# 64 KB rows in three slots, one softmax per head: a decode attention kernel and its loads regrouped

## The chip, the cores and the metric

The kernel runs on one core of one Trainium2 chip. The metric is the device time of one execution in microseconds (us). The kernel before takes 709.22 us, the median of three runs (712.56, 709.22 and 707.17).

## What is computed

One decode step of grouped-query attention with a cache, gated by a small MLP. There are 8 batches of one token each, 32 query heads and 8 key/value heads of width 128, and 4096 cached positions. All data are float32.

```
xn = layernorm(x)                                  # x: (8, 1, 512)
q  = (xn @ wq) as (batch, 32 heads, 1, 128)        # wq: (512, 4096)
s  = q . k_cache * 128**-0.5                       # k_cache: (8, 8, 4096, 128), one kv head per 4 q heads
o  = softmax(s) . v_cache                          # v_cache: (8, 8, 4096, 128)
a  = o as (batch, 1, 4096) @ wo                    # wo: (4096, 512)
z  = gelu(xn @ w_in)                               # w_in: (512, 1792), z1 and z2 are its halves
y  = (z1 * (w_sp * layernorm(z2) + b_sp)) @ w_out  # w_out: (896, 512)
out = x + a * silu(y)
```

The two caches are 268.4 MB (2 x 8 x 8 x 4096 x 128 x 4 bytes); wq, wo, w_in and w_out are 8.39, 8.39, 3.67 and 1.84 MB. Each byte is read once.

## The kernel before

The work goes through 64 pairs of a kv head `h` and a batch `b`, heads outermost. A pair needs one K tile and one V tile of 2 MB: 128 partitions with a row of 16 KB each. Both come from the pool `kv` with six buffers. K lies in memory with the head dimension on the partitions (its layout is made on the host); V lies with positions on the partitions.

For a pair, `scores` (L203) multiplies the 4 query vectors of the pair (a 128x4 stationary operand) with K, in four column groups g of 32 output partitions each, of which 4 are used, and two chunks c of 512 positions. The result is one PSUM tile of 128x1024, whose 16 used rows hold 4 query heads x 4 groups. VectorE takes the negated maximum of each row (L205), ScalarE the exponential with the sum of each row (L207). `transposed` turns the result with eight 128x128 transposes on TensorE (L216) and copies the 16 used columns out (L217). `values` (L225) multiplies it with V, 32 times for a pair, and L227 copies the 128x128 result out. Since every row has its own maximum, `factors` rescales the four groups once a head (L232 to L249), `combine` sums them with a matmul for each batch (L254), and `project_o` adds the head's share of the output projection into `acc` (L261).

What TensorE executes is written in a loop with one pair of delay: the scores of pair i come ahead of the transposes and values of pair i-1 in program order. TensorE runs its matmuls in that order. The last three pairs (`TAIL`) are handled apart in `finish_last`: their scores come first, and the last V tile comes in eight pieces.

All large loads are issued from one queue (SP) in program order: K and V of a pair, `wo` of the head at b = 2 and `wq` of the next head at b = 4 (1 MB each, in rows of 2 KB), `w_in` at pair 9 and `w_out` at pair 12. A load into a `kv` buffer waits on SP until TensorE has read the tile that was there, and each load waits for one of eight completion semaphores (named DMAHW0 to DMAHW7 below), which are used in turn. Whatever follows on SP waits behind. The query projection of head h+1 stands after pair b = 6 (L119), the MLP after pairs 11 and 14 (L144, L184).

In the profile a float32 matmul counts as two instructions, so the 8 matmuls of a pair's scores are x16 and the 32 of its values x64.

## Time and profile before

| what | value |
|---|---|
| median of three runs | 709.22 us (707.17 to 712.56) |
| span of the profiled execution | 707.2 us |
| TensorE busy (matmul) | 497.6 us, 70% |
| VectorE, ScalarE busy | 149.0 us, 80.6 us |
| packets of the SP queue, as a share of 16 DMA engines | 98.4% |
| bytes read | 290.80 MB |
| mean TensorE clock granted | 0.81 |

The profile shows one execution by its span, from the first to the last instruction. No other time of that execution is shown, so the span is its own time here; it is the same as the fastest of the three runs (707.17 us) and 2.0 us under their median. Busy time is the union of an engine's instructions, so four matmuls that run beside each other in four column groups count once. A packet is one contiguous row that one of the 16 DMA engines moves, or the few bytes that count up a semaphore; the share of a queue is the sum of its packets' durations over 16 times the time looked at. Since the groups of a stage overlap with loads for others, the busy shares alone don't say which engine sets the time.

### The profile page before, as it was taken

To read this page: it belongs to the slowest core of one execution; us is meant where nothing else is said; L and a number is where in the kernel's file an instruction comes from. 1 tells how busy PE (TensorE), PEld (TensorE's weight loads), DVE (VectorE), ACT (ScalarE), POOL (GpSimd) and SP (SyncE) were. 2 spreads that over 40 slices of the span, in tenths; PEclk is the share of its full clock that TensorE was granted. 3 is DMA by queue.
4 is the path that set the end of the run, shared out by engine and by line. 5 is a ranking of instruction groups with operands and counts; after the bars stand their busy time and mean duration, and the time that the engine had idled before them with its cause. 6 is when DMAs were issued, how large, how long until landed. Compare 5 with 4: busy or idle time off the path is not lost.

```text
span 707.2 us, 14005 instructions
## 1 busy us (share of the span) xinstructions
PE 497.6 (70%) x6480; PEld 305.9 (43%) x6480; DVE 149.0 (21%) x364; ACT 80.6 (11%) x139; POOL 3.1 (0%) x10
## 2 busy tenths in 40 slices
PE   6656777787868668776867668686477764878666
PEld 4323454573534345344534334444144432545334
DVE  2211122112222221222122211222112221122231
ACT  0110101001010110011011100111010111001120
POOL 0000000000000000000000000000000000000000
PEclk9967788856777996789778977978877897677999
DMA  8999999999999999999999999999999999999994
GB/s 336 429 419 422 426 428 422 423 406 427 425 394 376 416 428 428 426 421 420 427 428 425 423 419 426 429 418 425 423 427 426 419 422 426 426 426 423 427 395 170
DMA packets 31178, 291.77 MB, mean 413 GB/s; under 512 B 2952, under 2 KB 3208, under 8 KB 14864
## 3 DMA queue, kind: packets, MB, share of 16 engines
q1 hardware_dynamic: 30672, 290.79, 98.4%
q8 instruction: 51, 0.84, 0.5%
q10 hardware_dynamic: 448, 0.08, 0.1%
q14 instruction: 7, 0.06, 0.0%
HBM read 290.80 MB, written 0.07 MB: 411 GB/s over the span
## 4 chain that ended last, share of the span: by engine, by line
PE 49%; DMA 33%; DVE 9%; ACT 7%; issue 1%; ACTq 0%; DVEq 0%; SPq 0%
DMA kv<-in_kT 30%; PE sc L203 16%; PE o_ps L225 14%; PE scr L216 8%; DVE nm L205 7%; ACT p L207 6%; PE scr L119 4%; PE scr L144 3%; DMA kv<-in_v 2%; PE scr L254 2%; DMA xg_sb<-in_xg 1%; PE acc L261 1%; PE scr L184 0%; PE scr L245 0%; DVE o_sb L227 0%
## 5 line engine op out<-in xcount | busy, mean ns | idle before, releaser
L216 PE MATMUL scr<-ident,p 128*128 128x128 f32 x512 | 85.3, 320 | 145.2 <-ACT p L207 144.6
L203 PE MATMUL sc<-kv,qT 128*4 128x512 f32 x1024 | 154.9, 732 | 27.5 <-DMA kv<-in_kT 27.2
L225 PE MATMUL o_ps<-kv,pT 128*4 128x128 f32 x4096 | 169.0, 332 | 1.7 <-DMA kv<-in_v 1.6
L216 PEld LDWEIGHTS scr<-ident,p 128*128 128x128 f32 x512 | 66.6, 162 | 210.4 <-ACT p L207 208.3
L225 PEld LDWEIGHTS o_ps<-kv,pT 128*4 128x4 f32 x4096 | 120.6, 103 | 42.4 <-DVE pT L217 8.0
L207 ACT ACTIVATE p<-sc,nm 128x1024 f32<-128x1024 f32 x64 | 71.2, 1113 | 535.3 <-DVE nm L205 476.3
L205 DVE TENSOR_REDUCE nm<-sc 128x1 f32<-128x1024 f32 x64 | 78.4, 1225 | 172.0 <-PE sc L203 172.0
L203 PEld LDWEIGHTS sc<-kv,qT 128*4 128x4 f32 x1024 | 26.3, 95 | 90.8 <-issue 56.2
L217 DVE COPY pT<-scr 128x64 f32<-128x64 f32 x128 | 28.6, 224 | 155.9 <-PE scr L216 155.9
L227 DVE COPY o_sb<-o_ps 128x128 f32<-128x128 f32 x64 | 18.7, 292 | 152.7 <-PE o_ps L225 152.7
L119 PEld LDWEIGHTS scr<-xnT,wq_sb 128*128 128x128 f32 x256 | 35.9, 227 | 2.3 <-issue 2.0
L119 PE MATMUL scr<-xnT,wq_sb 128*128 128x8 f32 x256 | 36.7, 284 | 0.3 <-DVE xnT L113 0.3
L254 PEld LDWEIGHTS scr<-f,o_sb 128*128 128x128 f32 x128 | 22.8, 267 | 19.1 <-issue 11.5
L254 PE MATMUL scr<-f,o_sb 128*128 128x4 f32 x128 | 24.3, 312 | 6.1 <-DVE f L249 5.3
L144 PEld LDWEIGHTS scr<-xnT,w_in_sb 128*128 128x128 f32 x112 | 19.0, 271 | 0.2 <-issue 0.2
L144 PE MATMUL scr<-xnT,w_in_sb 128*128 128x8 f32 x112 | 19.1, 315 | 0.0
L261 PE MATMUL acc<-wo_sb,oT 128*8 128x128 f32 x256 | 11.0, 327 | 4.8 <-DVE oT L258 4.8
L207 ACT ACTIVATION_READ_ACCUMULATOR p<-sc,nm 128x1 f32 x64 | 12.3, 193 | 0.0
L261 PEld LDWEIGHTS acc<-wo_sb,oT 128*8 128x8 f32 x256 | 7.0, 103 | 6.5 <-DVE oT L258 5.5
L122 DVE TENSOR_SCALAR qT<-scr 128x32 f32<-128x32 f32 x8 | 1.5, 192 | 34.0 <-PE scr L119 34.0
L245 PE MATMUL scr<-wl,same 128*128 128x8 f32 x16 | 2.9, 252 | 6.3 <-DVE wl L243 6.3
L241 ACT ACTIVATE w<-w 128x8 f32<-128x8 f32 x8 | 1.7, 208 | 37.5 <-DVE w L240 37.5
(67 smaller groups left out, 45.2 us busy)
## 6 DMA issues: line engine op xcount, KB each, us to landing
kv<-in_kT SPq DMA_DIRECT2D x62, 2048.0 KB, 23.8
kv<-in_v SPq DMA_DIRECT2D x61, 2048.0 KB, 21.3
wq_sb<-in_wq SPq DMA_DIRECT2D x8, 1024.0 KB, 23.1
wo_sb<-in_wo SPq DMA_DIRECT2D x8, 1024.0 KB, 22.7
kv<-in_kT SPq DMA_DIRECT2D x4, 1024.0 KB, 15.5
kv<-in_v SPq DMA_DIRECT2D x8, 512.0 KB, 16.6
w_in_sb<-in_w_in SPq DMA_DIRECT2D x4, 896.0 KB, 23.6
kv<-in_v SPq DMA_DIRECT2D x8, 256.0 KB, 7.0
```

Of the source, the lines that this page charges most:

```text
L119: nc.tensor.matmul(pq[:, r * B:(r + 1) * B], wq_sb[:, k, r * DH:(r + 1) * DH], xnT[:, k, :], start=(k == 0), stop=(k == NK - 1))
L144: nc.tensor.matmul(pz[:, f * B:(f + 1) * B], w_in_sb[:, k, f * P:(f + 1) * P], xnT[:, k, :], start=(k == 0), stop=(k == NK - 1))
L203: nc.tensor.matmul(s[32 * g:32 * g + REP, c, :], qT[:, b, :], k_sb[:, c, g, :], start=True, stop=True)
L205: nc.vector.tensor_reduce(nm[:, b:b + 1], s, op=ALU.max, axis=AX.XY, negate=True)
L207: nc.scalar.activation(p.rearrange("p j s -> p (j s)"), s.rearrange("p c s -> p (c s)"), AF.Exp, bias=nm[:, b:b + 1], accum_out=l[:, b:b + 1])
L216: nc.tensor.transpose(t[:, j * P:(j + 1) * P], p[:, 4 * c + j, :], ident)
L217: nc.vector.tensor_copy(pT[:, 4 * c:4 * c + 4], t.rearrange("p (j g r) -> p j g r", j=4, g=G)[:, :, :, :REP])
L225: nc.tensor.matmul(o_ps[32 * g:32 * g + REP, :], pT[:, j, g, :], v_sb[:, j, g, :], start=(j == 0), stop=(j == J - 1))
L227: nc.vector.tensor_copy(o_sb[:, b, :], o_ps)
L245: nc.tensor.matmul(tot, same.rearrange("p g r -> p (g r)"), wl, start=True, stop=True)
L254: nc.tensor.matmul(po[:, b * REP:(b + 1) * REP], stats[h][2][:, b, :], f[:, b, :], start=True, stop=True)
L261: nc.tensor.matmul(acc[32 * g:32 * g + B, :], oT[:, r, :], wo_sb[:, r, g * P:(g + 1) * P], start=(h == 0 and r == 0), stop=(h == HKV - 1 a ...
```

## The change

The caches are laid out anew on the host, so that one load brings four batches of K, or of V, of a head: 8.4 MB, 128 rows of 64 KB. The tile pool becomes a ring of three slots of 64 KB a partition, and everything large goes through it. `w_in` and `w_out` share the first slot, whose unused part also holds the MLP's intermediate tiles; all of `wq` is the second; then follow, for each head, K in two halves and V in two halves; all of `wo` is the last, in six pieces of 16, 8, 4, 2, 1 and 1 of its 32 rows of 2 KB a partition. The last V half comes in four pieces.

The MLP and the query projection of all heads are computed first. They now use the small operand `xnT`, padded to 32 columns, as the stationary one, and the weights as the moving one. The queries are written into `qz`, where the four queries of batch b stand in columns 4b to 4b+3 of a 32-column block that is zero elsewhere. So the scores of all eight batches add up into one PSUM tile `sc` whose 32 rows of a column group hold 8 batches x 4 heads, and one softmax a head serves all of them: one maximum, one exponential, eight transposes. The rescaling is applied to `p` ahead of its transposes. `combine` runs once a V half, and the output projection runs once at the end.

On SP, the start of the program, with the semaphores that each load waits for. Before (a `kv` tile is a K or V tile of a pair):

```order
L44 DMA wq_sb_122<-in_wq 128x4x512
L56 DMA kv_143<-in_kT 128x2048 x2
L64 DMA kv_146<-in_v 128x4096
L56 DMA kv_162<-in_kT 128x4096 [waits DMAHW0_49]
L64 DMA kv_164<-in_v 128x4096 [waits DMAHW1_49]
L56 DMA kv_223<-in_kT 128x4096 [waits DMAHW2_49]
L64 DMA kv_225<-in_v 128x4096 [waits DMAHW3_49]
L49 DMA wo_sb_227<-in_wo 128x4x512 [waits DMAHW4_49]
L56 DMA kv_286<-in_kT 128x4096 [waits DMAHW6_49,DMAHW5_49,PE_49]
```

And now (slot_77, slot_80 and slot_340 are the first use of the three slots):

```order
L56 DMA slot_77<-in_w_in 128x7168
L57 DMA slot_77<-in_w_out 112x4096
L67 DMA slot_80<-in_wq 128x16384
L257 DMA slot_340<-in_kT 128x16384
L257 DMA slot_374<-in_kT 128x16384 [waits DMAHW1_49,DMAHW3_49,DVE_49,PE_49]
L264 DMA slot_442<-in_v 128x16384 [waits DMAHW4_49,PE_49]
L264 DMA slot_580<-in_v 128x16384 [waits DMAHW5_49,DMAHW0_49,PE_49]
L257 DMA slot_718<-in_kT 128x16384 [waits DMAHW6_49,PE_49]
```

Four loads (22.3 MB) are now issued without a wait; the fifth waits for the MLP, which reads and writes the first slot, the sixth for the query projection, the seventh for the scores of the first K half.

On SP, the end of the program. Before, the last V tile in eight pieces of 2 KB rows:

```order
L64 DMA kv_4526<-in_v 128x1024 [waits DMAHW7_49]
L64 DMA kv_4542<-in_v 128x512 [waits DMAHW0_49,PE_49]
L64 DMA kv_4542<-in_v 128x512 [waits DMAHW1_49]
L64 DMA kv_4542<-in_v 128x512 [waits DMAHW2_49]
L64 DMA kv_4542<-in_v 128x512 [waits DMAHW3_49]
```

And now, from the last V half on:

```order
L264 DMA slot_3226<-in_v 128x4096 [waits DMAHW1_49,PE_49]
L264 DMA slot_3226<-in_v 128x4096 x3
L280 DMA slot_3231<-in_wo 128x8192 [waits DMAHW2_49,PE_49]
L280 DMA slot_3231<-in_wo 128x4096
L280 DMA slot_3231<-in_wo 128x2048
L280 DMA slot_3231<-in_wo 128x1024 [waits DMAHW3_49]
L280 DMA slot_3231<-in_wo 128x512 [waits DMAHW4_49]
L280 DMA slot_3231<-in_wo 128x512 [waits DMAHW5_49]
L299 DMA out_0<-res_3514 128x128 [waits DMAHW6_49,DVE_49]
```

The pieces of wo wait for semaphores of loads that lie three and more loads back (DMAHW3 is that of the first V half of the last head, DMAHW4 and DMAHW5 those of the first two pieces of the second), where a piece of the last V tile before waited for the load eight places ahead of it.

On TensorE, the stretch from one pair to the next before, in the middle of the program:

```order
L203 MATMUL sc0_97<-kv_471,qT_141 4x512 x8
L216 MATMUL scr_567<-ident_83,p_484 128x128 x4
L216 MATMUL scr_573<-ident_83,p_484 128x128 x4
L225 MATMUL o_ps_99<-kv_473,pT_566 4x128 x32
L203 MATMUL sc1_98<-kv_551,qT_141 4x512 x8
```

And now all of one head:

```order
L203 MATMUL sc_98<-slot_340,qz_91 32x512 x32
L203 MATMUL sc_98<-slot_374,qz_91 32x512 x32
L213 MATMUL scr_411<-ident_82,nm_122 1x128
L219 MATMUL scr_417<-ident_82,full_415 128x1
L226 MATMUL scr_424<-wl_422,same_93 128x1
L234 MATMUL scr_430<-ident_82,p_409 128x128 x4
L234 MATMUL scr_436<-ident_82,p_409 128x128 x4
L242 MATMUL o_ps0_99<-slot_442,pT_429 4x128 x128
L251 MATMUL scr_574<-same_93,o_sb_572 128x4 x4
```

A head has as many matmuls for scores (64) and values (256) as before, but 8 transposes where there were 64, and no score of the next head stands ahead of this head's values.

The diff, cut:

```diff
-TAIL = 3
+R = 32
+HALF = B // 2
+UNIT = 2 * G * 512
+SLOT = HALF * UNIT
+WO_PIECES = [(0, 16), (16, 24), (24, 28), (28, 30), (30, 31), (31, 32)]
...
-    wpool = ctx.enter_context(tc.tile_pool(name="wpool", bufs=2))
-    kv = ctx.enter_context(tc.tile_pool(name="kv", bufs=6))
-    work = ctx.enter_context(tc.tile_pool(name="work", bufs=2))
+    ring = ctx.enter_context(tc.tile_pool(name="ring", bufs=3))
+    work = ctx.enter_context(tc.tile_pool(name="work", bufs=1))
...
+    def slot():
+        return ring.tile([P, SLOT], F32, name="slot")
...
+    nc.sync.dma_start(mlp_slot[:, :NK * 2 * FH], w_in)
+    nc.sync.dma_start(w_out_sb, w_out)
...
+    wq_sb = slot()
+    nc.sync.dma_start(wq_sb, wq)
...
+    qz = const.tile([P, HKV, B * R], F32, name="qz")
+    nc.gpsimd.memset(qz, 0.0)
...
+    def mlp():
+        z = from_slot(P, 2 * FQ).rearrange("p (a f) -> p a f", a=2)
+        pz = scratch([P, 2 * FQ], "pz")
+        for part in range(2):
             for k in range(NK):
+                for g in range(G):
+                    lo = part * FH + g * FQ
+                    nc.tensor.matmul(pz[R * g:R * (g + 1), part * FQ:(part + 1) * FQ], xnT[:, k, :],
+                                     w_in_sb[:, k, lo:lo + FQ], start=(k == 0), stop=(k == NK - 1))
...
+    def project_q(quad):
+        pq = scratch([P, REP * DH], "pq")
+        for k in range(NK):
             for g in range(G):
+                lo = (quad * G + g) * REP * DH
+                nc.tensor.matmul(pq[R * g:R * (g + 1), :], xnT[:, k, :], wq_sb[:, k, lo:lo + REP * DH],
+                                 start=(k == 0), stop=(k == NK - 1))
+        q_sb = work.tile([P, REP * DH], F32, name="q_sb", tag="p")
+        nc.vector.tensor_scalar(q_sb, pq, float(DH) ** -0.5, None, op0=ALU.mult)
+        tq = scratch([P, REP * P], "tq")
+        for r in range(REP):
+            nc.tensor.transpose(tq[:, r * P:(r + 1) * P], q_sb[:, r * DH:(r + 1) * DH], ident)
...
+                nc.vector.tensor_copy(qz[:, h, o:o + REP], tv[:, :, g, b])
...
+    def scores(h, half, k_sb):
+        for i in range(HALF):
+            b = half * HALF + i
+            for c in range(2):
+                for g in range(G):
+                    nc.tensor.matmul(sc[R * g:R * (g + 1), c, :], qz[:, h, b * R:(b + 1) * R],
+                                     k_sb[:, i, c, g, :], start=(b == 0), stop=(b == B - 1))
+
+    def softmax(h):
+        m = nm[:, h:h + 1]
+        nc.vector.tensor_reduce(m, sc, op=ALU.max, axis=AX.XY, negate=True)
+        p = work.tile([P, J, P], F32, name="p")
+        nc.scalar.activation(p.rearrange("p j s -> p (j s)"), sc.rearrange("p c s -> p (c s)"), AF.Exp,
+                             bias=m, accum_out=l[:, h:h + 1])
+        a = scratch([1, P], "a")
+        nc.tensor.transpose(a, m, ident)
...
+        nc.vector.tensor_scalar(p, p, w, None, op0=ALU.mult)
+        pT = work.tile([P, J, P], F32, name="pT")
         for c in range(2):
             t = scratch([P, 512], "t")
             for j in range(4):
                 nc.tensor.transpose(t[:, j * P:(j + 1) * P], p[:, 4 * c + j, :], ident)
+            nc.vector.tensor_copy(pT[:, 4 * c:4 * c + 4, :].rearrange("p j s -> p (j s)"), t)
...
+    def load_k(h, half):
+        t = slot()
+        nc.sync.dma_start(t, kT[h, half])
...
+    mlp()
+    project_q(0)
+    project_q(1)
+    for h in range(HKV):
+        for half in range(2):
+            scores(h, half, load_k(h, half))
+        pT = softmax(h)
+        for half in range(2):
+            last = h == HKV - 1 and half == 1
+            v_sb = load_v(h, half, HALF if last else 1)
+            if last:
+                wo_slot = slot()
+                for lo, hi in WO_PIECES:
+                    nc.sync.dma_start(wo_slot[:, lo * D:hi * D], wo[:, lo * D:hi * D])
+            o = o_ps[half]
+            for i in range(HALF):
+                values(half * HALF + i, pT, v_sb[:, i], o)
+                if last:
+                    combine(h, half * HALF + i, 1, o)
+            if not last:
+                combine(h, half * HALF, HALF, o)
...
+    for m in range(HKV * REP):
+        h, r = divmod(m, REP)
+        for g in range(G):
+            nc.tensor.matmul(acc[R * g:R * g + B, :], oT[:, h, r, :], wo_sb[:, m, g * P:(g + 1) * P],
+                             start=(m == 0), stop=(m == HKV * REP - 1))
...
+        "kT": c(k.transpose(2, 0, 7, 1, 4, 6, 5, 3)).reshape(HKV, 2, P, SLOT),
+        "v": c(vv.transpose(2, 0, 3, 1, 4, 5, 6)).reshape(HKV, 2, P, SLOT),
+        "wq": c(c(A_wq).reshape(NK, P, HKV * REP * DH).transpose(1, 0, 2)).reshape(P, SLOT),
+        "wo": c(c(A_wo).reshape(HKV * REP, P, D).transpose(1, 0, 2)).reshape(P, SLOT),
```

More of the change, by code (lines that the diff above doesn't have):

```diff
@@ L85, in tile_gqa_gmlp_decode @@
         nc.vector.tensor_copy(same[:, g, :], same[:, 0, :])
-    sc = [ps_fix.tile([P, 2, 512], F32, name=f"sc{i}") for i in range(2)]
-    o_ps = ps_fix.tile([P, DH], F32, name="o_ps")
+    same_all = same.rearrange("p g r -> p (g r)")
+    sc = ps_fix.tile([P, 2, 512], F32, name="sc")
+    o_ps = [ps_fix.tile([P, HALF, DH], F32, name=f"o_ps{i}") for i in range(2)]
     acc = ps_fix.tile([P, P], F32, name="acc")
-    for t in (sc[0], sc[1], o_ps, acc):
+    for t in (o_ps[0], o_ps[1], acc):
         nc.vector.memset(t, 0.0)
@@ L126, in tile_gqa_gmlp_decode @@
[L126 to L148 removed]
+    nc.vector.tensor_copy(xnT[:, :, :B], pt.rearrange("p (k b) -> p k b", k=NK))
@@ L253, in combine @@
-    def combine(h, b, f, po):
-        nc.tensor.matmul(po[:, b * REP:(b + 1) * REP], stats[h][2][:, b, :], f[:, b, :], start=True, stop=True)
-    def project_o(h, po, wo_sb):
-        oT = small.tile([P, REP, B], F32, name="oT")
-        nc.vector.tensor_copy(oT, po.rearrange("p (b r) -> p r b", r=REP))
-        for r in range(REP):
-            for g in range(G):
-                nc.tensor.matmul(acc[32 * g:32 * g + B, :], oT[:, r, :], wo_sb[:, r, g * P:(g + 1) * P],
-                                 start=(h == 0 and r == 0), stop=(h == HKV - 1 and r == REP - 1))
@@ L320, in tile_gqa_gmlp_decode, with combine @@
-    finish_last(tail)
+                lo = R * g + REP * b
+                nc.tensor.matmul(o[R * g:R * g + REP, b % HALF, :], pT[:, j, lo:lo + REP],
+                                 v_unit[:, j, g, :], start=(j == 0), stop=(j == J - 1))
+    def combine(h, b0, n, o):
+        o_sb = small.tile([P, HALF, DH], F32, name="o_sb")
+        i0 = b0 % HALF
+        nc.vector.tensor_copy(o_sb[:, i0:i0 + n], o[:, i0:i0 + n])
+        po = scratch([P, n * REP], "po")
+        for i in range(n):
+            nc.tensor.matmul(po[:, i * REP:(i + 1) * REP], o_sb[:, i0 + i, :], same[:, 0, :REP],
+                             start=True, stop=True)
+        nc.vector.tensor_copy(oT[:, h, :, b0:b0 + n], po.rearrange("p (b r) -> p r b", r=REP))
@@ L322, in tile_gqa_gmlp_decode @@
+    wo_sb = wo_slot.rearrange("p (m d) -> p m d", d=D)
+    for m in range(HKV * REP):
+        h, r = divmod(m, REP)
+        for g in range(G):
+            nc.tensor.matmul(acc[R * g:R * g + B, :], oT[:, h, r, :], wo_sb[:, m, g * P:(g + 1) * P],
+                             start=(m == 0), stop=(m == HKV * REP - 1))
     res = const.tile([P, P], F32, name="res")
     nc.vector.tensor_mul(res, acc, gate)
-    nc.vector.tensor_add(res, res, xg_sb)
+    nc.vector.tensor_add(res, res, side_sb[:, :P])
```

302 lines of the change are left out of this document (96 added, 206 removed).

## Prediction

> **What bounds the kernel now.** I read the page first: its span, the share of the SP queue and the chain of the work that ended last.
>
> ```profile
> span 707.2 us, 14005 instructions
> ...
> q1 hardware_dynamic: 30672, 290.79, 98.4%
> ...
> PE 49%; DMA 33%; DVE 9%; ACT 7%; issue 1%; ACTq 0%; DVEq 0%; SPq 0%
> ```
>
> The queue's packets fill 98.4% of the 16 engines' time. The chain seems to say otherwise: half of it is TensorE. But it goes back at each step to whatever released that step, and a load that waits for its buffer leads it to TensorE even while the engines still work through loads queued earlier. The waits on SP show that this is so:
>
> ```profile
> SPq L64 <- PE o_ps L225: 284.2, 51, 7.7
> SPq L56 <- PE sc L203: 168.7, 55, 9.9
> ```
>
> SP waits 453 us of the span for TensorE to free a `kv` buffer. Whether that costs anything is told by the bytes moved, in a table of stretches (columns: length; busy time of PE, PEld, DVE, ACT, POOL; clock; DMA share; GB/s):
>
> ```profile
> 0.00:10.00 10.00, 4.18 (x21) 4.09 (x22) 4.21 (x13) 1.28 (x1) 1.43 (x9) 1.00 0.81 296
> 200.00:230.00 30.00, 23.71 (x309) 13.78 (x308) 6.77 (x19) 2.62 (x5) 0.00 (x0) 0.74 0.95 378
> 230.00:680.00 450.00, 315.32 (x4292) 189.46 (x4292) 94.93 (x222) 54.12 (x94) 0.00 (x0) 0.81 1.01 424
> 690.00:701.00 11.00, 8.62 (x186) 6.08 (x188) 2.30 (x11) 0.21 (x1) 0.00 (x0) 1.00 0.70 251
> 701.00:707.20 6.20, 1.81 (x42) 1.14 (x42) 1.07 (x4) 0.00 (x0) 0.00 (x0) 0.98 0.05 15
> ```
>
> From 230 to 680 us the engines are full at 424 GB/s: the six buffers hide SP's waits. Losses are 3 us at the start (10 x (1 - 296/424)), 3.3 us from 200 to 230 us (30 x (1 - 378/424)), 4.5 us in 690 to 701 (11 x (1 - 251/424)) and the 6.2 us behind. So the kernel is bound by its transfers, and the question is what a byte costs in the new rows.
>
> **The price of a packet.** Two stretches of different mix give it, by the transfer view of each. 70 to 80 us moves rows of 16 KB alone; 300 to 315 us moves one load in 2 KB rows as well:
>
> ```profile
> DMA packets 292, 4.26 MB, mean 426 GB/s; under 512 B 32, under 2 KB 32, under 8 KB 32
> ...
> q1 hardware_dynamic: 292, 4.26, 100.1%
> ```
>
> ```profile
> DMA packets 895, 6.31 MB, mean 421 GB/s; under 512 B 62, under 2 KB 62, under 8 KB 574
> ...
> q1 hardware_dynamic: 894, 6.29, 101.1%
> ```
>
> First: 100.1% of 16 x 10 us over 260 data packets (292 less 32 semaphore counts) is 616 ns for 16 KB. Second: 101.1% of 16 x 15 us is 242.6 us; 320 packets of 16 KB (894 - 62 - 512) take 197.1, and the 512 of 2 KB (574 - 62) the other 45.5, 88.9 ns each. The line through both is 13.6 ns a packet and 36.77 ns a KB of 1000 bytes. With it, the program's packets before (15,744 of 16 KB, 512 of 8 KB, 512 of 7 KB, 1,024 of 4 KB, 10,112 of 2 KB) come to 691.8 us an engine, against 98.4% of 707.2 = 695.9.
>
> **The change: loads.** No packet over 16 KB is in the trace. On the line, 64 KB take 2,423 ns (433 GB/s over 16 engines); as four of 16 KB they'd take 2,464. I take the line, as it holds from 2 to 16 KB. Per engine, eight rows a load:
>
> - 31 K and V halves of 64 KB rows: 248 x 2.423 = 600.9 us
> - last V half in four pieces: 32 x 0.616 = 19.7
> - wq: 8 x 2.423 = 19.4
> - w_in (28 KB rows): 8 x 1.068 = 8.5; w_out (112 rows of 16 KB): 7 x 0.616 = 4.3
> - wo: 8 x (1.218 + 0.616 + 0.315 + 0.164 + 2 x 0.089) = 19.9
>
> Together 672.8 us, 19.0 under the 691.8 of before on the same line. The 10,112 packets of 2 KB, nearly all gone, carry 8.4 of it (256 stay: 9,856 x 13.6 ns / 16).
>
> **The change: does the ring keep up?** A slot is 19.4 us of transfer, two slots are queued behind the one being read, so a half must be consumed within 38.8 us of its landing. Rows of TensorE across a head's end, with both clocks in them (start, duration):
>
> ```profile
> 290.82 0.27 PE L232 MATMUL scr<-ident,nm 128*8 128x128 f32 x1
> 291.83 0.20 PE L238 MATMUL scr<-ident,full 8*128 8x8 f32 x1 [0.74 <-DVE full L236]
> 292.81 0.36 PE L245 MATMUL scr<-wl,same 128*128 128x8 f32 x2 [0.79 <-DVE wl L243]
> 293.90 2.72 PE L254 MATMUL scr<-f,o_sb 128*128 128x4 f32 x12 [0.73 <-DVE f L249]
> 296.55 3.60 PE L203 MATMUL sc<-kv,qT 128*4 128x512 f32 x16
> 300.08 0.91 PE L254 MATMUL scr<-f,o_sb 128*128 128x4 f32 x4
> 301.59 1.06 PE L261 MATMUL acc<-wo_sb,oT 128*8 128x128 f32 x32 [0.61 <-DVE oT L258]
> 302.79 1.09 PE L216 MATMUL scr<-ident,p 128*128 128x128 f32 x8
> 303.82 1.93 PE L225 MATMUL o_ps<-kv,pT 128*4 128x128 f32 x64
> 305.56 1.90 PE L203 MATMUL sc<-kv,qT 128*4 128x512 f32 x16
> ```
>
> ```profile
> L207 ACT ACTIVATE p<-sc,nm 128x1024 f32<-128x1024 f32 x64 | 71.2, 1113 | 535.3 <-DVE nm L205 476.3
> L205 DVE TENSOR_REDUCE nm<-sc 128x1 f32<-128x1024 f32 x64 | 78.4, 1225 | 172.0 <-PE sc L203 172.0
> ...
> L144 PE MATMUL scr<-xnT,w_in_sb 128*128 128x8 f32 x112 | 19.1, 315 | 0.0
> ```
>
> At the slow clock throughout, a K half is 4 x 3.60 = 14.4 us and a V half 4 x 1.93 x 2 = 15.4 (estimate, scaled as L203). The softmax now stands between them with nothing overlapping: 1.2 maximum, 1.1 exponential, 3.1 from L232 to L254, at most 1.2 for scaling `p` (the maximum's size), 1.1 transposes, at most 1.2 for two copies of half that size: 9 us. Two combines add 3. A head is at most 28.8 + 9 + 30.8 + 3 = 72 us, against 32 x 2.423 = 77.5 us of transfer. TensorE idles, and each half is gone within 20 us of landing. The saved work (56 of 64 transposes, maxima and exponentials a head) therefore earns nothing by itself, and all else on these engines is priced at nothing, covered by the transfers; without that cover it would be the softmax's 9 us a head.
>
> The start is tighter. The fifth load (queued behind the fourth) waits for the MLP, and all of SP behind it. w_in is there at 3 + 8.5 = 11.6 us; POOL's clearing of `qz`, ahead of the layer norm's power, hides behind that transfer. The MLP's form is new: 64 instructions of 224 columns are at most 4 x 3.6 = 14.4 us (L203's of 512); above nothing, and the 19.1 of L144 if it gains nothing. A dozen vector steps of 448 columns or fewer are at most 1.2 each, the gate and the rest some 8. So the slot is free by 35 to 53 us; it is wanted when the first K half ends, at 3 + 8.5 + 4.3 + 19.4 + 19.4 = 54.6. wq is wanted back 19.4 us later, and its 64 instructions (14.4 at most) start at 35. The third slot has more.
>
> **The change: the end.** The last rows before:
>
> ```profile
> 700.96 0.40 PE L225 MATMUL o_ps<-kv,pT 128*4 128x128 f32 x8 [0.24 <-DMA kv<-in_v]
> ...
> 703.57 0.29 DVE L323 TENSOR_TENSOR res<-acc,gate 128x128 f32<-128x128 f32 x1 [1.18 <-PE acc L261]
> ...
> 704.33 0.35 SPq L325 DMA_DIRECT2D out<-res  x1
> ```
>
> Behind the last load stood 2.6 us of values, combine and projection and 3.6 us of gate and output. Now eight instructions of the projection (0.4, as the row at 700.96) and the same 3.6. The last V pieces came at 251 GB/s, each waiting for a semaphore eight loads back; the wo pieces are queued early, so I charge them the line, plus 1.5 us for the last landing and for engines that don't end together.
>
> **The sum.** Start 3.0 + transfers 672.8 + 1.5 + 0.4 + 3.6 = 681.3 us of span. The profiled execution lay 2.0 us under the median of its runs, so 683.3. Against before: 19 us of packets, 2.2 of tail, the rest gaps.
>
> **Rivals.**
>
> *Longer rows earn nothing.* The engines may handle 64 KB in pieces as dear as 16 KB: 256 x 41 ns (2,464 - 2,423) = 10.4 us more, 694. For it: nothing longer was seen; against it: the line. The Trainium skill, "DMA: Bandwidth & Descriptors", section on bandwidth, measured 425 GB/s for a transfer of 16 MB; by that, as an estimate, 290.7 MB are 684 us and the sum 695. This trace already holds 424 with 2 KB rows mixed in.
>
> *The rows slow the memory; this is the one that ends slower.* The engines' rows now start 64 KB apart, not 16, so they may strike the same part of the memory together. Price: beyond 716.3 us if the stream takes 705.7, that is a 64 KB packet of 2,551 ns or more (5% over the line); at 400 GB/s (2,621 ns) it is 734. A loss of 3 to 5% stays within 1% of now. For it: no load with such a distance is in the trace; against it: rows 2 KB (wo), 7 KB (w_in) and 16 KB apart (wq, K, V) already mix in the 424 GB/s of 230 to 680 us or ahead of it, and no stretch with all buffers full falls behind for it. The skill's page on DMA, section on latency and other measured facts, has copies losing 3% at 512 KiB from row to row, half at 4 MiB; 3% here would be an estimate of 705. No run here shows it, and 64 KB lies far below.
>
> *The column groups no longer run side by side* with 32-column operands: 16 instructions in 4 x 1.90, a K half 30.4, a head at the full clock 88 us against 77.5, in all 86 us more: 769. Against it: groups have the same 32 output partitions as before.
>
> *The start holds the ring*: were the MLP 10 us beyond its bound, 693, once.
>
> **How the numbers follow.** Forecast (676 to 690) 0.58; rows earn nothing 0.24; start 0.05; memory 3 to 5% slower 0.06, more than that 0.05; column groups 0.02. Under 702.1 us (faster by over 1%, about what a measurement can tell) lie the first three and a little of the fourth: 0.88; within 1%: 0.06; slower 0.06. The range 676 to 700 holds the first three cases.
>
> **What would show it.** Right: 430 GB/s or more in all slices but the ends, under 6,000 packets, SP's waits long yet harmless, TensorE waiting for loads at each half, about 5.5 us behind the last packet. Wrong: 425 GB/s throughout (rows earn nothing); under 415 (memory); empty slices near 55 us (start); matmuls of the scores filling the span (column groups).

## The result, and the profile after

The changed kernel takes 689.97 us (median of four runs, 689.83 to 690.91). The kernel before took 708.82 us beside it (707.17 to 712.56). The ratio is 0.9725, with a 95% interval of 0.9684 to 0.9767: faster by 2.7%. The forecast was 683.3 us with a range of 676 to 700, so the sign and the range hold, and the number itself is 6.7 us too low.

The profiled execution took 690.91 us with a span of 689.0, so a run's time is its span and 1.9 us around it. So the execution with a span of 707.2 us before, too, was one of about 709 us and not the fastest of its runs. The forecast took its 2.0 us to be the luck of one execution; it is this offset, and its size was right.

The page of the changed kernel: its size, the bandwidth in 40 slices, and the queues (q1 carries the loads that SP issues; q8 fetches TensorE's instructions, q14 those of GpSimd and others).

```profile
span 689.0 us, 12056 instructions
...
GB/s 310 434 426 431 430 431 447 428 434 423 438 436 423 435 438 439 436 427 430 427 436 443 434 430 429 428 434 431 428 439 431 441 431 428 428 427 441 410 432 206
...
q1 hardware_dynamic: 6464, 290.79, 98.3%
q8 instruction: 45, 0.74, 0.4%
```

q1 now has 6,464 packets, where it had 30,672. All slices but the ends stand between 410 and 447 GB/s, and the dip to 378 from 200 to 230 us is gone. The stretches of the changed kernel (columns as in the prediction: length; busy time of PE, PEld, DVE, ACT, POOL; clock; DMA share; GB/s):

```profile
0.00:10.00 10.00, 0.59 (x4) 0.50 (x4) 3.46 (x12) 1.28 (x1) 3.17 (x10) 1.00 0.85 326
10.00:20.00 10.00, 5.12 (x64) 3.06 (x64) 1.06 (x2) 0.00 (x0) 0.00 (x0) 1.00 1.12 331
20.00:640.00 620.00, 336.08 (x4954) 178.61 (x4955) 60.32 (x193) 12.14 (x26) 0.56 (x1) 0.73 1.00 433
640.00:670.00 30.00, 22.34 (x534) 17.43 (x532) 3.92 (x11) 0.00 (x0) 0.00 (x0) 0.79 0.98 418
670.00:683.00 13.00, 7.42 (x195) 5.85 (x194) 0.17 (x1) 0.00 (x0) 0.00 (x0) 0.74 0.74 310
683.00:689.00 6.00, 2.39 (x72) 1.37 (x64) 0.58 (x2) 0.00 (x0) 0.00 (x0) 1.00 0.15 53
```

The body runs at 433 GB/s, the rate of the forecast. 291.63 MB (the loads and the fetches of instructions) at 433 are 673.5 us. Measured against that rate, the stretches lose 2.5 us (10 x (1 - 326/433)), 2.4, nothing, 1.0, 3.7 and 5.3 us: 14.9. The kernel before needs three stretches beside those that the prediction shows:

```profile
10.00:20.00 10.00, 7.13 (x33) 3.85 (x34) 1.42 (x2) 1.21 (x2) 0.00 (x0) 1.00 0.96 394
20.00:200.00 180.00, 129.18 (x1528) 84.18 (x1528) 35.10 (x88) 17.68 (x31) 1.66 (x1) 0.76 1.01 423
680.00:690.00 10.00, 7.69 (x78) 3.36 (x79) 3.16 (x6) 3.53 (x6) 0.00 (x0) 1.00 0.98 381
```

By the same measure it loses 4.1 us up to 20 us, 4.2 from 20 to 200, 3.8 from 200 to 230, 9.4 from 230 to 680, 1.2 from 680 to 690, and 10.6 behind that: 33.3. Up to 20 us and from 680 us on that is 15.9 (4.1 + 1.2 + 10.6), where the changed kernel loses all its 14.9 up to 20 us and from 640 us on. So the gain of 18.2 us of span lies almost wholly in the body, 17.4 us of it.

SP still waits long for TensorE, and the start went as computed. The waits of SP (total us, times, longest), and rows of the start (start, duration, idle time before in brackets):

```profile
SPq L257 <- PE o_ps L242: 80.1, 7, 13.3
SPq L264 <- PE o_ps L242: 79.6, 7, 12.6
SPq L264 <- PE sc L203: 72.8, 8, 9.9
...
SPq L257 <- DVE gate L173: 21.7, 1, 21.7
```

```profile
13.72 5.12 PE L124 MATMUL scr<-slot,xnT 128*32 128x224 f32 x64 [8.37 <-DMA slot<-in_w_in]
34.99 0.29 DVE L173 TENSOR_TENSOR gate<-scr,slot 128x128 f32<-128x128 f32 x1
40.50 5.80 PE L180 MATMUL scr<-slot,xnT 128*32 128x512 f32 x32 [7.49 <-DMA slot<-in_wq]
```

The MLP's 64 matmuls take 5.1 us, the gate is there at 35.3 us, and by the forecast's count its slot is wanted at 54.6. So SP's wait of 21.7 us for `gate` costs nothing, as the 433 GB/s from 20 us on show. The last rows of the changed kernel:

```profile
665.93 3.46 PE L242 MATMUL o_ps<-slot,pT 128*4 128x128 f32 x64 [0.43 <-DMA slot<-in_v]
...
675.76 8.30 PE L293 MATMUL acc<-slot,oT 128*8 128x128 f32 x224 [5.58 <-DMA slot<-in_wo]
...
685.47 0.41 PE L293 MATMUL acc<-slot,oT 128*8 128x128 f32 x8 [0.20 <-DMA slot<-in_wo]
685.94 0.29 DVE L297 TENSOR_TENSOR res<-acc,gate 128x128 f32<-128x128 f32 x1 [15.56 <-PE acc L293]
...
686.59 0.35 SPq L299 DMA_DIRECT2D out<-res  x1
```

Behind the last `wo` piece stand the forecast's 0.4 us of matmuls and 3.1 us to the end. The last piece itself lands 8 us later than forecast (685.4 us against 681.3 - 4.0 = 677.3).

### The profile page after: what moved, and what is told of

Its sections match the earlier page's. It is cut to its first block, busy times and chain, and to the rows that moved or that the text cites. A ratio compares the mean times of both kernels' runs of the same rounds, so it can differ in the third digit from the quotient of the medians.

```text
span 689.0 us, 12056 instructions
## 1 busy us (share of the span) xinstructions
PE 373.9 (54%) x5810; PEld 206.8 (30%) x5810; DVE 69.5 (10%) x220; ACT 13.4 (2%) x27; POOL 3.7 (1%) x11
## 2 busy tenths in 40 slices
DMA packets 6672, 291.63 MB, mean 423 GB/s; under 512 B 744, under 2 KB 1000, under 8 KB 1392
## 3 DMA queue, kind: packets, MB, share of 16 engines
q1 hardware_dynamic: 6464, 290.79, 98.3%
## 4 chain that ended last, share of the span: by engine, by line
DMA 71%; PE 20%; another core or an unknown queue 5%; issue 2%; DVE 1%; SPq 0%
DMA slot<-in_v 47%; DMA slot<-in_kT 14%; PE o_ps L242 11%; PE sc L203 7%; DMA slot<-in_wq 6%; DMA slot<-in_wo 4%; PE scr L180 1%; PE scr L251 1%; DVE o_sb L248 0%; DVE q_sb L183 0%; PE scr L186 0%; PE acc L293 0%; SPq L57 0%; SPq L56 0%
## 5 line engine op out<-in xcount | busy, mean ns | idle before, releaser
L203 PE MATMUL sc<-slot,qz 128*32 128x512 f32 x1024 | 145.8, 733 | 131.8 <-DMA slot<-in_kT 131.8
L242 PE MATMUL o_ps<-slot,pT 128*4 128x128 f32 x4096 | 153.7, 318 | 96.3 <-DMA slot<-in_v 70.8
L242 PEld LDWEIGHTS o_ps<-slot,pT 128*4 128x4 f32 x4096 | 117.1, 99 | 130.6 <-issue 60.4
L203 PEld LDWEIGHTS sc<-slot,qz 128*32 128x32 f32 x1024 | 35.7, 132 | 235.4 <-DMA slot<-in_kT 132.6
L208 DVE TENSOR_REDUCE nm<-sc 128x1 f32<-128x1024 f32 x8 | 9.8, 1225 | 274.3 <-PE sc L203 274.3
L251 PE MATMUL scr<-same,o_sb 128*128 128x4 f32 x128 | 21.6, 288 | 13.4 <-DVE o_sb L248 12.6
L251 PEld LDWEIGHTS scr<-same,o_sb 128*128 128x128 f32 x128 | 19.9, 233 | 19.7 <-DVE o_sb L248 18.9
L210 ACT ACTIVATE p<-sc,nm 128x1024 f32<-128x1024 f32 x8 | 8.9, 1113 | 590.8 <-DVE nm L208 590.8
L234 PE MATMUL scr<-ident,p 128*128 128x128 f32 x64 | 14.5, 402 | 10.7 <-DVE p L229 10.7
L234 PEld LDWEIGHTS scr<-ident,p 128*128 128x128 f32 x64 | 11.5, 207 | 11.1 <-issue 11.1
L235 DVE COPY pT<-scr 128x512 f32<-128x512 f32 x16 | 11.1, 692 | 10.4 <-PE scr L234 10.4
```

The costliest lines, as they stand in the source:

```text
L203: nc.tensor.matmul(sc[R * g:R * (g + 1), c, :], qz[:, h, b * R:(b + 1) * R], k_sb[:, i, c, g, :], start=(b == 0), stop=(b == B - 1))
L208: nc.vector.tensor_reduce(m, sc, op=ALU.max, axis=AX.XY, negate=True)
L210: nc.scalar.activation(p.rearrange("p j s -> p (j s)"), sc.rearrange("p c s -> p (c s)"), AF.Exp, bias=m, accum_out=l[:, h:h + 1])
L234: nc.tensor.transpose(t[:, j * P:(j + 1) * P], p[:, 4 * c + j, :], ident)
L235: nc.vector.tensor_copy(pT[:, 4 * c:4 * c + 4, :].rearrange("p j s -> p (j s)"), t)
L242: nc.tensor.matmul(o[R * g:R * g + REP, b % HALF, :], pT[:, j, lo:lo + REP], v_unit[:, j, g, :], start=(j == 0), stop=(j == J - 1))
```

## The experiments

The numbers in front of a bracket are medians in us, the bracket is the range of the runs. The kernels ran in five sets, with the kernel before in each of them: its medians are 708.8 to 710.6, its single runs 707.0 to 715.1. The changed kernel ran in the first set alone. It and its variants scatter by 0.1 to 0.25% within a set; kernels of different sets are compared by their medians, so a difference of less than about 1 us between sets shows nothing by itself.

### The price of a packet: rows cut to 16 KB and to 4 KB

Each load still brings 8.4 MB, with K and V laid out so that a 64 KB row of a partition comes as four rows of 16 KB, or sixteen of 4 KB:

```diff
-        nc.sync.dma_start(t, kT[h, half])
+        nc.sync.dma_start(t.rearrange("p (c n) -> p c n", c=4), kT[h, half].rearrange("c p n -> p c n"))
```

> The changed kernel with K and V laid out on the host so that a load's 64 KB a partition come as four rows of 16 KB from four places; slots, loads, waits and all computation stay. My theory (a packet costs 13.6 ns and 36.77 ns a KB, so longer rows earn by fewer packets): 256 long packets an engine become 1,024 of 616 ns, +10.4 us, 700.4 us. Rival (longer rows earn nothing; the gain is from the saved work and the gaps): 690.

> The same with sixteen rows of 4 KB for each row of 64 KB (4,096 packets an engine in place of 256). My theory: 16 x 164.2 ns = 2,627 in place of 2,423, 256 x 204 ns = +52 us, 742 us. Rival (rows of 4 KB and more cost by the byte alone): 690.

Measured: 693.58 (693.13 to 693.66) with 16 KB and 707.96 (707.62 to 708.36) with 4 KB. Neither theory's size holds. Cutting adds 744 packets an engine (31 loads x 8 rows x 3, since the last V half has rows of 16 KB in the changed kernel too) and 3.6 us, or 3,816 packets and 18.0 us: 4.9 and **4.7 ns a packet**, about a third of the 13.6 that the prediction read from before. The two cut kernels ran in one set, and the 3,072 packets and 14.4 us between them are 4.7 ns as well. The body of the 16 KB kernel, and then that of the 4 KB one with its queue:

```profile
20.00:640.00 620.00, 330.42 (x4947) 173.74 (x4947) 57.35 (x184) 10.88 (x24) 0.56 (x1) 0.72 1.01 430
```

```profile
20.00:640.00 620.00, 319.07 (x4882) 171.86 (x4882) 55.98 (x182) 10.58 (x23) 0.56 (x1) 0.72 1.02 420
```

The DMA share (the last column but one) tells what was wrong with the reading: it is 1.02, the sum of the packets' durations being more than the engines' time. So packets that follow each other on an engine overlap in the records, the more the shorter they are, and a price from their durations counts the overlap as cost. The medians of the durations over a whole run say the same thing:

```
row                        64 KB   16 KB    8 KB    4 KB    2 KB
median ns, kernel after     2418     611     309     159      84
median ns, kernel before               613     313     159      85
```

Four of 16 KB are 26 ns more than one of 64, 8.7 ns for each packet more; the elapsed time charges 4.7.

### The saved softmaxes: one, or eight in a row

The changed kernel has one maximum and one exponential a head. Here each is done eight times, one after the other, as often as before:

```diff
+        for _ in range(B):
-        nc.vector.tensor_reduce(m, sc, op=ALU.max, axis=AX.XY, negate=True)
+            nc.vector.tensor_reduce(m, sc, op=ALU.max, axis=AX.XY, negate=True)
```

(and the exponential behind it likewise).

> The changed kernel with the maximum and the exponential of a head done eight times in a row, as often as before the change: 7 x (1.23 + 1.31) = 17.8 us more a head on VectorE and ScalarE, between the scores and the values. My theory (the saved work earns nothing, the transfers cover it; a half may be consumed within 38.8 us of its landing and is by some 27 without it): up to +2 us, 690 to 692. Rival (one softmax a head is what makes the kernel faster): 8 x 17.8 = +142 us, 832.

Measured: 696.76 (695.72 to 697.44), 6.8 us more than the changed kernel. Neither number was met. The body and the end of this kernel:

```profile
200.00:640.00 440.00, 239.97 (x3774) 134.37 (x3774) 79.43 (x112) 51.62 (x90) 0.00 (x0) 0.74 1.00 432
```

```profile
655.65 0.75 DVE L230 TENSOR_SCALAR p<-p,w 128x1024 f32<-128x1024 f32 x1
...
682.69 1.93 PE L243 MATMUL o_ps<-slot,pT 128*4 128x128 f32 x64
...
685.35 7.17 PE L294 MATMUL acc<-slot,oT 128*8 128x128 f32 x256
```

The body keeps 432 GB/s with six times the ScalarE time, so in the first seven heads the saved work earns nothing, as forecast. The price is paid in the last head alone: seven more rounds of 2.5 us delay its values, which end at 684.6 us instead of 669.4, and all 256 instructions of the projection then run after the last `wo` piece has landed (684.5 us), with no load left beside them. The transfers cover the softmax of every head but the last: 15.2 us later there (684.6 - 669.4) cost 6.8, so that head has some 8.4 us of slack.

### The start: `w_out` in 128 rows

`w_out` has 112 rows, seven for each of the 16 engines if they share them evenly. From 10 to 20 us, where it is moved, the changed kernel has 331 GB/s at a DMA share of 1.12. In the layout of this experiment 16 rows of zeros fill it up:

```diff
-    nc.sync.dma_start(w_out_sb, w_out)
+    nc.sync.dma_start(w_out_all, w_out)
...
+        "w_out": np.concatenate([..., np.zeros((P - FB, NB * D), np.float32)]),
```

> The changed kernel with w_out loaded as 128 rows (16 rows of zeros behind its 112). From 10 to 20 us the changed kernel moves 331 GB/s at a share of 1.12: packets there take longer than their bytes. Theory (112 rows, seven to an engine, make engines stand in each other's way): the stretch returns to 433 GB/s, -2.4 us, plus 0.6 us for 0.26 MB more: 688.2. Rival (it is the start as such, or the small rows of side): +0.6, 690.6.

Measured: 687.82 (687.70 to 688.24), a ratio of 0.9682 to before (0.9652 to 0.9712). It moves 0.26 MB more and is 2.15 us faster than the changed kernel, as the first theory expected. It computes the whole output, and is the fastest version here that does.

```profile
10.00:20.00 10.00, 4.95 (x64) 2.97 (x64) 2.27 (x4) 0.27 (x1) 0.00 (x0) 1.00 1.09 466
```

466 GB/s in place of 331. In the trace the 16 KB packets of the whole changed kernel have a mean of 675 ns, and 613 here. 112 of the former's 752 are `w_out`'s; if the others take 613, those take (752 x 675 - 640 x 613) / 112 = 1,030 ns. Taken by their start (before 20 us), the 112 have a mean of 1,027 ns, and the 128 of this kernel 611. In these two kernels the rows of a load of 112 take two thirds longer than those of a load of 128. Why, no run here shows.

### Longer rows or larger loads

With 4.7 ns a packet, two parts of the change can be priced apart. Here the slots stay, but each half comes in four loads of 2 MB with 16 KB rows, as large as the loads before:

```diff
-        nc.sync.dma_start(t, kT[h, half])
+        n = SLOT // 4
+        for c in range(4):
+            nc.sync.dma_start(t[:, c * n:(c + 1) * n], kT[h, half, c])
```

> The changed kernel with K and V in rows of 16 KB as in the first run of rows, and each half brought by four loads of 2 MB (128 rows of 16 KB each), the shape of the loads before the change; slots and computation stay. Theory (only packets and their few semaphore counts matter): 693.6 as with one load of four rows, plus 96 loads x 9 ns, 694.5. Rival (large loads, or their semaphore waits on SP, make the gain of the body of the program): well above, up to 703.

Measured: 694.20 (693.90 to 694.50), as expected from the packets. Loads four times larger earn at most 0.6 us beside what their rows earn, and that is no more than two sets may differ by. Rows and loads of K and V together are worth 4.2 us of the gain.

The same for `wq` and `wo`. In the first kernel, the changed one gets them in rows of 2 KB again; in the second, the one before gets them in rows of 8 KB:

```diff
-    nc.sync.dma_start(wq_sb, wq)
+    nc.sync.dma_start(wq_sb.rearrange("p (c n) -> p c n", c=32), wq.rearrange("c p n -> p c n"))
```

> The changed kernel with wq and wo in rows of 2 KB, as many as before the change (7,936 packets more, some 490 an engine), in the same loads and slots. By 4.7 ns of time a packet (what rows of 16 KB and 4 KB of K and V gave): +2.3 us, 692.3. By the prediction's 13.6 ns: +6.7, 696.7. Rival (2 KB rows of weights hold the kernel before back by far more): 700 or above.

```diff
-        nc.sync.dma_start(t, wq_v[:, :, h * REP * DH:(h + 1) * REP * DH])
+        nc.sync.dma_start(t.rearrange("p k n -> p (k n)"), wq[h])
```

> The kernel before with one part of the change alone: wq and wo laid out on the host so that their loads of 1 MB come in rows of 8 KB, not 2 KB (6,144 packets fewer, 384 an engine). By the price of a packet that the two runs with shorter rows gave (4.7 ns of time): -1.8 us, 708.5 against 710.3. By the prediction's 13.6 ns: -5.2 us, 705. Rival (rows of 2 KB are what holds the kernel before to 424 GB/s where the changed one has 433): -9 us or more, 701.

Measured: 692.08 (691.70 to 692.32, and one run of 701.31), 2.1 us more, as 4.7 ns a packet has it. And 708.18 against 710.51 of the kernel before, 2.3 us less, at a ratio of 0.9971 (0.9941 to 1.0000); here the runs scatter by 7.7 us, so alone it would prove little. The two agree.

### The dip from 200 to 230 us: the MLP moved to the start of the kernel before

The kernel before with 8 KB rows still dips where the MLP's loads stand:

```profile
200.00:230.00 30.00, 24.61 (x316) 14.96 (x314) 6.17 (x19) 2.62 (x5) 0.00 (x0) 0.72 0.95 375
```

In the next kernel its MLP is loaded and computed ahead of the first pair, and nothing else is changed:

```diff
+    w_in_sb, w_out_sb = load_mlp_in(), load_mlp_out()
     wq_t[0] = load_wq(0)
+    mlp_gate(mlp_hidden(w_in_sb), w_out_sb)
     qT[0] = project_q(wq_t[0])
...
-        if i == 9:
-            mlp["in"] = load_mlp_in()
```

> The kernel before with wq and wo in rows of 8 KB (as in the run of that) and, besides, the MLP loaded and computed ahead of the first pair; K, V, slots and the softmax of each pair stay. Theory (in the kernel before, TensorE is 20 us late after the MLP, the six buffers run dry and 200 to 230 us lose 3.8 us against 433 GB/s): that stretch goes back to 424 and above, 708.2 - 4 = 704, less what a start with more queued saves. Rival (the stretch has another cause): 708, and the loss stays where it is.

Measured: 712.97 (710.21 to 716.04), 1.0026 of before (1.0002 to 1.0049) and 4.8 us more than the kernel with 8 KB rows that it is built on: no gain, where 704 was expected. Its stretches, a row of its start, and a wait of SP:

```profile
20.00:40.00 20.00, 17.32 (x81) 17.07 (x80) 1.93 (x8) 0.30 (x1) 0.00 (x0) 1.00 1.02 428
40.00:60.00 20.00, 13.13 (x130) 8.53 (x134) 5.43 (x17) 1.51 (x3) 1.66 (x1) 0.87 0.83 338
60.00:100.00 40.00, 26.79 (x468) 16.50 (x464) 9.82 (x20) 6.02 (x10) 0.00 (x0) 0.93 0.97 403
100.00:680.00 580.00, 408.34 (x5480) 243.35 (x5472) 120.59 (x285) 67.71 (x117) 0.00 (x0) 0.82 1.01 426
```

```profile
13.89 22.78 PE L142 MATMUL scr<-xnT,w_in_sb 128*128 128x8 f32 x106 [2.46 <-DMA w_in_sb<-in_w_in]
```

```profile
SPq L54 <- PE sc L201: 207.3, 60, 28.6
```

The dip is gone from 200 us and has come back at 40 to 100 us (338 and 403 GB/s). The MLP's old form holds TensorE for 23 us, while the six `kv` buffers fill; the first of them comes free only when the first scores are done, and SP waits 28.6 us for that. In the changed kernel the new form of 64 wide instructions takes 5.1 us, and nothing is lost from 20 us on. So the dip goes where the MLP goes, and moving the old form to the start earns nothing. That the new form is what makes the early place free is an inference: no run has one without the other.

### The end: what makes the engines finish apart

The changed kernel's largest loss is at its end. Each load is spread over all 16 DMA engines, and each engine counts up the load's semaphore when its part has landed. The trace has the times of these counts (16 for each of the 45 loads, 720 in all), but not which engine made them. For some loads of the changed kernel, the first of the 16, and how far the last is behind it:

```
first (us)   96.4   193.1   289.7   386.3   482.8   579.4   618.1
spread (us)   1.8     3.1     4.6     4.7     6.1     7.6     7.6
the 16 at 618 us, behind the first: 0 0 0.1 0.1 0.3 0.4 1.5 1.6 6.5 7.0 7.1 7.1 7.2 7.4 7.5 7.6
```

Half of the engines keep step; the other eight fall behind in steps of about 1.4 us and never catch up, as each engine has its part of every load. The fast ones move a load in 19.3 us throughout (579.4 - 96.4 over 25 loads). What happens now and then is q8's fetch of 16 KB of TensorE's instructions: 45 of them, 39 up to 618 us, and 39 x 1.4 / 8 engines would be 6.8 us. In the trace, 2,606 of the 2,634 packets of 64 KB that start from 100 to 500 us take 2.41 to 2.43 us, and the other 28 take 2.88 to 2.97; none lies between. Of the 27 fetches in that time, each has one such long packet beside it, and takes 0.88 to 0.99 us itself: with the half microsecond by which the long packet is longer, this is the step of 1.4. The first test leaves most of the values out:

```diff
-        for j in range(J):
+        for j in range(2):
```

> The changed kernel with a quarter of the values: only 2 of the 8 position blocks j are multiplied with V, so the output leaves out the rest; all loads stay. TensorE has 6,144 instructions fewer, of 12,056. Theory (the code is itself fetched by DMA, 45 packets of 16 KB, each holds up one engine by some 1.3 us, and half of the engines fall behind by 7.6 us by the end, which the others wait out): some 23 fetches fewer, the lag at the end about 3.5 us, -4 us, 686. Rival (the lag is a matter of the engines or of memory, and TensorE's work is covered): 690.

Measured: 685.97 (685.42 to 686.67), 4.0 us less, as expected.

```profile
span 684.1 us, 5912 instructions
...
q8 instruction: 21, 0.34, 0.2%
```

6,144 instructions less are 24 fetches less (256 instructions each), and the spread at 618 us is 4.7 instead of 7.6 us; the last `wo` piece lands at 680.5 and not 685.4 us. TensorE's work was off the critical path; still its instructions cost time, by way of the engines that load them. But less work on TensorE could matter in another way too, so the next test adds instructions on an engine that has nothing to do. GpSimd clears one element 4,096 times, and nothing waits for it:

```diff
     mlp()
+    idle = const.tile([1, 1], F32, name="idle")
+    for _ in range(4096):
+        nc.gpsimd.memset(idle, 0.0)
```

> The changed kernel with 4,096 clearings of one element on GpSimd, which nothing waits for (some 0.1 us each, 410 us on an engine that is otherwise idle after the MLP). Theory (it is the code's own fetches that hold up half of the transfer engines): 4,096 instructions of 64 bytes (0.74 MB for 12,056 instructions is 61 each) are 16 more fetches of 16 KB, 45 become 61, the lag at the end grows from 7.6 to about 10 us, +2.7 us, 692.7. Rival (the run with a quarter of the values was faster because TensorE did less): 690.

Measured: 704.77 (704.53 to 705.14), 14.8 us more than the changed kernel. The direction is that of the theory, the size five times larger. The page of this kernel, the group of the added instructions, and two of its stretches:

```profile
span 702.9 us, 16152 instructions
...
q8 instruction: 45, 0.74, 0.4%
q14 instruction: 35, 0.29, 0.1%
```

```profile
L270 POOL MEMSET idle<- 1x1 f32 x4096 | 369.0, 90 | 236.1
```

```profile
20.00:640.00 620.00, 323.00 (x4882) 174.26 (x4882) 57.21 (x185) 10.73 (x23) 359.69 (x3991) 0.72 1.00 431
...
690.00:702.90 12.90, 7.34 (x239) 5.69 (x228) 0.58 (x2) 0.00 (x0) 0.00 (x0) 0.93 0.07 25
```

q14 had 3 packets and now has 35: 32 fetches of 8 KB. By the counts they all fall on one engine:

```
first (us)                       309.2   386.7   464.1   541.5   619.1
one engine behind the first       11.5    14.2    16.8    19.4    21.4
next slowest behind the first      4.8     5.1     6.4     7.9     8.1
```

That one engine loses 0.65 us a load, about one fetch's worth in every 19 us, until GpSimd is done; the others are as they were. GpSimd is done at 609.6 us; 32 fetches of 0.65 us are 20.8 of the 21.4. The body hardly feels it (431 GB/s), but the last load is complete only when this engine has done its share: 25 GB/s from 690 us to the end, one engine at work and fifteen idle. Expected was the same lag spread over eight engines. The clearings themselves don't slow the loads: the packets of 64 KB from 100 to 500 us still take 2.41 to 2.43 us, 2,570 of 2,619, and nearly all of the others are again those beside a fetch, 2.9 us or so beside one of q8 and mostly 2.77 beside one of q14. So instructions that no one waits for, on an engine that is otherwise idle, lengthen the kernel by what their fetches take from one DMA engine, once that engine is the slowest.

Two more runs tried to give the slow engines less to do. A load of eight rows is counted eight times and not 16 (the second of these kernels has 800 counts, 42 x 16 + 16 x 8), so it uses eight engines. In the first, `w_out` (in 128 rows) comes in 16 such loads on ScalarE's queue; in the second, the last six of the 32 rows of `wo` on a partition, on SP, behind pieces of 16, 6 and 4 rows:

```diff
-    nc.sync.dma_start(w_out_all, w_out)
+    for p0 in range(0, P, 32):
+        for i in range(4):
+            lo = p0 + i
+            nc.scalar.dma_start(w_out_all[lo:lo + 29:4], w_out[lo:lo + 29:4])
```

> The changed kernel with w_out padded to 128 rows and brought by 16 loads of eight rows, four partitions apart, on ScalarE's queue, so that, if a load of eight rows uses eight engines and always the same, these carry 1.05 MB more and the other eight 1.05 MB less than their share (4.8 us each way). Theory: at the end eight engines are 7.6 us behind the others; if the eight that get more are those ahead, the end comes some 4 us earlier than with even rows (687.8): 684; if they are those behind, 4 to 5 us later: 692. Rival (loads of eight rows are spread evenly after all, or the lag is not tied to engines): 688 plus the dearer small loads, 688 to 690.

```diff
+                for p0 in range(0, P, 32):
+                    for i in range(p0, p0 + 4):
+                        nc.sync.dma_start(wo_slot[i:i + 29:4, hi * D:], wo[i:i + 29:4, hi * D:])
```

> The changed kernel with w_out padded to 128 rows and the last 6 of wo's 32 rows of 2 KB a partition brought by 16 loads of eight rows, four partitions apart, on SP behind everything else: if these use eight fixed engines, they move 3.7 us of transfers from the other eight to them at the very end. Theory: if the eight are those that are ahead by 7.6 us, the end comes up to 3.7 us earlier than 687.8, at 684 to 685; if they are those behind, as much later, 691 to 692. Rival (loads of eight rows are spread over all engines): 688.

The first measured 708.06 (707.31 to 708.43) and answers another question. Its issues on ScalarE's queue, SP's longest wait, and a stretch:

```profile
1.80 56.28 ACTq L61 DMA_DIRECT2D slot<-in_w_out  x16
```

```profile
SPq L261 <- DMA slot<-in_w_out: 43.2, 2, 42.6
```

```profile
53.00:71.00 18.00, 5.32 (x74) 4.55 (x78) 4.62 (x14) 1.86 (x2) 0.56 (x1) 0.50 0.16 66
```

These loads hold ScalarE for 56 us, and mostly not by being issued: an issue takes 0.63 us, 10 us for all 16, and the rest is waits for the semaphores of loads issued earlier. The MLP, which needs ScalarE, comes late (its gate at 73.4 us and not 35.3); SP waits 42.6 us for the landing of these loads and 12.2 for the gate, with all else behind it, and for 18 us the ring is dry at 66 GB/s. This is the forecast's rival "the start holds the ring" made real: about 20 us beside the kernel with `w_out` in 128 rows.

The second measured 695.66 (695.22 to 695.94), 7.8 us more than the kernel with `w_out` in 128 rows that it is built on, where the theory had a gain of 3.7 if the eight are the engines ahead, and a loss about as large if they are those behind. Its end:

```profile
663.12 22.14 SPq L284 DMA_DIRECT2D slot<-in_wo  x12
...
687.78 2.74 PE L297 MATMUL acc<-slot,oT 128*8 128x128 f32 x48 [7.42 <-DMA slot<-in_wo]
```

The last of the 16 loads lands at 687.6 us, 5.0 later than the last of the other kernel (682.6). The lag of the engines doesn't set this end; the waits of SP do. Each small load waits for the semaphore of the one eight places back, so the last eight are issued only from 679.5 us on, when the first has landed (679.2), one every 0.67 us until 685.3. From 680 to 685 us the DMA share is 0.43. Most of the remaining 2.8 us is TensorE's: six rows of `wo` are multiplied behind the last landing (2.7 us), not one (0.4). The counts do tell something of the first eight small loads: those of the first come at 670.6 to 672.6 us from six engines and at 677.3 and 679.2 us from two, so the eight engines used there are neither the eight that are ahead nor the eight that lag, and the run couldn't test its theory. Whether the end could be evened out by giving the engines that lag less to do stays open.

## Why the prediction was right and where it was wrong

**The bound: right.** The transfers set the time; SP's waits for TensorE are long and harmless; the body stands at 433 GB/s, the number that the line gave for 64 KB rows (2,423 ns forecast, 2,418 the median measured). That a 64 KB row is moved as well as a line through 2 and 16 KB has it was the choice on which the forecast rested.

**The price of a packet: too high by a factor of three.** This is a failed step: "the line through both is 13.6 ns a packet". It was read from durations that add up to 100.1% and 101.1% of the engines' time, and the 1.1% that the short packets overlap was taken as part of their cost. That isn't all of the error: with 100% in place of 101.1%, the 512 packets take 42.9 us, 83.8 ns each, and the line has 7.7 ns a packet. Cut rows cost 4.7 ns a packet; why the durations still overstate it is not shown. The kernel has 22,288 data packets less (27,904 before, 5,616 now), 1,393 an engine: 6.5 us of the gain and not the 19. The direct measurements agree: 4.2 us for K and V, 2.1 to 2.3 for `wq` and `wo`. The sum came near in spite of this, because 64 KB packets do take what the line says; only the comparison with before was flattered. In part this is luck. The line has 41 ns between four packets of 16 KB and one of 64 (2,464 and 2,423). With rows of 16 KB in the new program the four take 2,444 (4 x 611), so the longer row accounts for 26 ns; the rest is that 16 KB packets are shorter in the new program than the 616 ns read from before, which the forecast didn't foresee. Nor did the 19 us of packets make the gain of 18.2 us that comes so close to them. What else made up the body's gain of 17.4 us: 3.8 are the dip at 200 to 230 us, which goes with the MLP's place and form. In the trace, 16 KB packets from 240 to 640 us take 616.3 ns on average in the kernel before and 612.3 in the one with 2 MB loads in three slots, where nearly all take 611; on 984 packets an engine this is at most 3.9 us, and its cause was not tested. Some 3 us stay unassigned (17.4 - 6.5 - 3.8 - 3.9). So the runs price about 10 of the 17.4 us, and the cause of the rest is open.

**The end: 1.5 us forecast, 6.5 measured.** "1.5 us for the last landing and for engines that don't end together" is the step that put the number too low. The stretches from 640 us on lose 10.0 us, of which 3.5 lie behind the last landing; the sum had 5.5 (1.5 + 0.4 + 3.6). It knew nothing of a lag between engines, 7.6 us at 618 us and 9.0 at the last `wo` piece. The kernel with 6,144 instructions less and the one with 4,096 more show where it comes from.

**The start: 3.0 us forecast, 4.9 measured.** "w_out (112 rows of 16 KB): 7 x 0.616 = 4.3" is the mis-sized term: with the 1,030 ns a packet above it is 7.2. With 128 rows the time falls by 2.15 us.

These two, 4.5 us (10.0 - 5.5) and 1.9, and the transfers' 0.7 (673.5 and not 672.8) are 7.1 of the 7.7 us between the forecast's span of 681.3 and the 689.0 measured; the rest is within the rounding of 433, where half a GB/s is 0.7 us over the body.

**The ring: right.** The MLP's slot is free at 35.3 us, inside the bound of 35 to 53 and at its low end, since the new MLP form takes 5.1 us and not 14.4. No slice between 20 and 640 us falls back.

**The softmax: right in the body, incomplete at the end.** That the saved work earns nothing by itself is shown for seven heads. For the last one the cover is thin; eight softmaxes in a row cost 6.8 us there. The prediction named the price without cover but did not say that the last head has little of it.

**The tail: right.** It took 0.4 us of matmuls and 3.1 to the end, 3.5 in place of 4.0.

**The rivals.** "Longer rows earn nothing" is refuted, since cutting the rows costs time; its price of 10.4 us was too high, too: rows of 16 KB cost 3.6. The Trainium skill, "DMA: Bandwidth & Descriptors", section on bandwidth, has 425 GB/s for 16 MB; this core held 433 for 620 us with 64 KB rows and 420 with 4 KB rows, so the measurement decides and lies higher. "The rows slow the memory" is refuted by the same 433 GB/s with rows 64 KB apart. "The column groups no longer run side by side" is refuted too: the scores are 1,024 instructions with a mean of 733 ns in 145.8 us of busy time, which one after the other would be 751 us.

```profile
L203 PE MATMUL sc<-slot,qz 128*32 128x512 f32 x1024 | 145.8, 733 | 131.8 <-DMA slot<-in_kT 131.8
```

"The start holds the ring" did not happen, but the run with `w_out` on ScalarE's queue shows that it can, and what it costs. Of the things that would show the steps right, three were missed as they were worded. There are 6,672 packets in all against "under 6,000", since the counts of the semaphores (720 of 4 bytes) and the 160 packets of q10 were not in it. "430 GB/s or more in all slices but the ends" holds for the mean of 433 only: 13 of the 38 slices between the ends lie below 430, all but the one of 410 at 423 or more. And 3.5 us, not "about 5.5", stand behind the last landing, since what the engines' lag costs is lost ahead of it.

## What to carry to other kernels

Where the packets' share of the engines comes out over 100%, their durations overlap and are no price: cut the same bytes into other rows and take the difference of the times. In a kernel bound by loads that are spread over all DMA engines, the end waits for the slowest of them, so count what each engine carries besides the data: fetches of instructions, also those of engines that nobody waits for, and loads whose rows don't fill 128 partitions (here 112 rows cost 2.15 us). Work that transfers hide is free only until the last load; look at the last head by itself.

## What the runs showed of the hardware that was not expected

- **Instructions cost transfer time.** TensorE fetches 16 KB for 256 of its instructions, and each fetch sets one DMA engine back by about 1.4 us, more than twice what 16 KB of data take (0.61 us); the lags in the trace have about eight engines sharing them. GpSimd's fetches of 8 KB, one for 128 instructions, set back a single engine by about 0.65 us each. 32 of these cost 14.8 us, while 24 of TensorE's cost 4.0. The Trainium skill, "Runtime: NRT & Kernel Launch", section on instruction fetch mechanics, says that the sequencer fetches blocks of 16 KiB, 256 instructions, through a DMA queue of its own, and that the cost is mostly hidden. The 45 and 21 packets of q8 agree with the blocks, the 8 KB fetches of GpSimd don't; the 4.0 and the 14.8 us show that hidden from the sequencer is not hidden from the loads.
- **112 rows are slower than 128.** The smaller load of `w_out` makes the kernel 2.15 us longer, at 1,027 ns a 16 KB packet against 611.
- **A packet more costs 4.7 to 4.9 ns** in a queue that is always full, from 64 KB rows of K and V down to 4 KB, and for `wq` and `wo` in rows of 2 KB the 2.1 us fit the same price, so that 4 KB rows still stream 420 GB/s.
